# A longer warm-up and a new order of transforms, weight decodes and mixture steps in a one-core Fourier and MLP kernel

## The chip, the cores and the metric

The kernel runs on one core of a Trainium2 chip. The metric is the device time of one execution in microseconds, the median of several. A core has TensorE (PE, matmul), VectorE (DVE), ScalarE (ACT), GpSimd (POOL), SyncE (SP, which here issues the transfers) and 16 DMA engines.

## The reference, cut to what matters

For two batches of 3136 positions and 256 channels, in three parts:

```
X = rfft(x, axis=1)                                  # attention: a mixture in the Fourier domain
Yr, Yi = Xr@w_r - Xi@w_i + b_r, Xr@w_i + Xi@w_r + b_i
Y = sign(Y) * max(|Y| - 0.01, 0)                     # soft threshold, on both parts
y = irfft(Y, n=3136)
x1 = y + relu(layernorm(y) * g @ w_ch1) @ w_ch2      # first MLP, 256 -> 1024 -> 256
u = x1 + real(fft(fft(x1, axis=1), axis=2))          # second mixture
out = u + relu(layernorm(u) @ v_ch1) @ v_ch2         # second MLP
```

The weights of both MLPs arrive as 64-bit floating-point numbers, which the chip sees as integers.

## The kernel before, in words

The long transform is split into a contraction with 98 rows and short transforms of 64 points, and products that need more than the matmul's precision are made of a high and a low part (x h and x l), three matmuls each (L213 to L215, L219 to L221).

- **Forward** (class `Forward`, matmul L300, transpose L301): 16 groups of 512 columns for each batch. A group is one matmul with `cam`, two records in the trace, and one transpose by VectorE into `yg`. Batch 0 reads x through tiles h, batch 1 through tiles q. Ahead of all stand WARM_UP matmuls on zeros (L740).
- **Steps** (`p2_step`): 26 of them, 13 for each batch. `p2_b` makes the 64-point transform (L420) with the table `cb` and splits it into parts, `p2_mix` multiplies by `wm` (24 matmuls, L452) and applies bias and threshold (VectorE L458 and L459, then POOL L209), `p2_inv` transforms back (L472) with the table `cw`. `p2_mix` and `p2_inv` run some steps behind. STAGE1_AT says how many groups of batch 1's Forward stand in each step, STAGE3_AT how many groups of batch 0's Inverse, CONST_AT and MLP1_AT in which step a table is loaded and a weight piece decoded.
- **Inverse** (class `Inverse`): 16 groups for each batch: transpose by VectorE (L316), matmul (L318), copy by ACT (L201). After the last group the seven stores of dY follow (L324, L325), and the first MLP's loads of ya wait for them. Batch 1's groups run between tiles of the first MLP.
- **First MLP** (`run_mlp`, 13 chunks of 2 to 4 tiles): BN statistics (L549 to L551), normalization q (L562; POOL does some of it in chunk 0), transpose by TensorE with `ident` (L573) into psc and scaling (ACT L578, DVE L579), first layer (L219 to L221), activation (L597, L598), second layer (L213 to L215), sum with the input (L615), store dX. The prep of chunk 0 stands in the steps (PREP0_AT).
- **Second mixture** (class `Stage98`, one for each batch): `start` loads a middle column m and the first rows r, makes mhl (L204, L209) and mid, and splits two groups. Each of 16 `step`s loads a row group (L345), splits it on POOL (L357 to L359) and into s and its rest (ACT L201, DVE or POOL L209), multiplies (L219 to L221), and stores dA.
- **Second MLP**: 13 chunks, with `stage_b` (L674) and `dmix` (L699) as the second axis of the transform, weights `r2b`.
- **Weights**: `decode64` loads a piece of 512 KB (L489) and turns it into a high and a low part by eight VectorE operations (L495 to L503). There are eight pieces for each MLP; those of the second one are decoded during the first.

Within a program order that these tables set, a scheduler orders each engine's instructions by a simulated timeline. `hook` puts a function behind a given tile (chunk k, layer "l1" or "l2", tile i): decodes of the second weights (MLP2_AT, chunk and tile as the two digits), batch 1's inverse groups (STAGE3_MLP) and steps of the second mixture (STAGE4_FROM, STAGE4_AT). `s4[1]`, the mixture of batch 1, has a step behind each second-layer tile of chunks 0 to 3 of the second MLP.

Of the kernel before, what the change touches and what calls it, by code (L numbers as in the profile page):

```python
# [10 lines left out]
F32R = mybir.dt.float32r  # L11
I32 = mybir.dt.int32
# [3 lines left out]
YB, HB, WB, SB = 4, 9, 4, 2  # L16
R98, S98, O98 = 4, 8, 4


ZERO_AT = 12  # L20
STAGE1_AT = (0, 0, 0, 2, 2, 2, 2, 2, 2, 2, 2)
STAGE3_FROM = 16
STAGE3_AT = (0,) * 16 + (2, 2, 2, 2, 2, 2, 2, 2)
CONST_AT = (0, 0, 1, 2, 2, 3, 4, 5, 6, 8)
MLP1_AT = (5, 8, 10, 12, 13, 14, 15, 18)
MLP2_AT = (61, 65, 71, 75, 81, 85, 91, 95)
STAGE3_END = 3
STAGE3_MLP = ((0, 0), (0, 1), (0, 2), (0, 3), (1, 0), (1, 1), (1, 2), (1, 3),
              (2, 0), (2, 1), (2, 2), (2, 3), (3, 0))
# [1 line left out]
INV_BEHIND = 3  # L31
STAGE_B_AT = (1, 3)
DMIX_AT = (3, 5)
PREP0_AT = (26, 27)
L2_BEHIND = 7
PREP_BEHIND = (3, 2, 0)
APPLY_POOL = (0, 1)
APPLY_CHUNKS = 2
STAGE4_AT = ((7, "l2", 1), (7, "l2", 2), (7, "l2", 3), (8, "l1", 3), (8, "l1", 4), (8, "l2", 0),
             (8, "l2", 1), (8, "l2", 2), (8, "l2", 2), (9, "l1", 3), (9, "l2", 0), (9, "l2", 1),  # L40
             (9, "l2", 3), (10, "l1", 6), (10, "l2", 0), (10, "l2", 1), (10, "l2", 1), (10, "l2", 3))
STAGE4_FROM = (6, 4)
WARM_UP = 5
TB = 2
I64 = mybir.dt.int64
AF = mybir.ActivationFunctionType
# [115 lines left out]
def fourier_moe_kernel(ctx, tc, x, w_r, w_i, b_r, b_i, g_ln, w11, w12, w21, w22,  # L162
                       t_ca, t_cam, t_cim, t_cb, t_ci, t_cb0, t_ci0, t_cd, t_ident, out):
    nc = tc.nc
    sp = nc.sync

    cp = ctx.enter_context(tc.tile_pool(name="cp", bufs=1))
    wk = ctx.enter_context(tc.tile_pool(name="wk", bufs=2))
# [5 lines left out]
    def psum(tag):  # L174
        return pp.tile([128, 512], F32, tag="ps" + tag, name="ps" + tag, bufs=ps_bufs[tag])
# [24 lines left out]
    def a_copy(o, i, scale=1.0):  # L200
        nc.scalar.activation(out=o, in_=i, func=AF.Copy, scale=scale)  # L201
# [57 lines left out]
    wm = cp.tile([128, 2, 1024], F32R, tag="wm", name="wm")  # L259
# [5 lines left out]
    def behind(f):  # L265

        with ExitStack() as es:
            for k, ins in mark.items():
                if k != "pe":
                    es.enter_context(tc.issue_after(ins))  # L270
            f()
# [209 lines left out]
        p2_inv(i - INV_BEHIND)  # L481


    def decode64(src3, dh, dl, tag):


        s64 = wk.tile([128, 512], I64, tag=tag, name="s64", bufs=2)
        o = s64 if len(src3.shape) == 2 else s64.rearrange("p (f c) -> p f c", f=src3.shape[1])
        sp.dma_start(out=o, in_=src3)  # L489
        t = wk.tile([128, 2, 512], I32, tag="stg", name="t64", bufs=SB)  # L490
        w, low = s64.bitcast(I32)[:, 1::2], s64.bitcast(U32)[:, 0::2]
        t1, t2 = t[:, 0, :], t[:, 1, :]
# [12 lines left out]
    def load_mlp(w1, w2, r, tag):

        def piece(src, o):
            def f():
                decode64(src, r[:, 0, o:o + 512], r[:, 1, o:o + 512], tag)
            return f  # L510

        fs = []
        for i in range(4):
            c, h = divmod(i, 2)
            fs.append(piece(w1[c * 128:(c + 1) * 128, h * 512:(h + 1) * 512], i * 512))
        for i in range(4):
            fs.append(piece(w2[i * 256:(i + 1) * 256, :].rearrange("(f p) c -> p f c", p=128), 2048 + i * 512))
        return fs

    def w_views(r):  # L520
        return ([r[:, i, 0:2048].rearrange("p (k f) -> p k f", k=2) for i in range(2)],
                [r[:, i, 2048:].rearrange("p (f c) -> p f c", f=NF) for i in range(2)])
# [233 lines left out]

    def split_wm():
        for m in range(2):
            ms = slice(m * 512, (m + 1) * 512)
            a_copy(wm[:, 0, ms], wm_raw[:, ms])  # L760
            sub(nc.vector, wm[:, 1, ms], wm_raw[:, ms], wm[:, 0, ms])

    def l_bias():
        for h, bv in enumerate((b_r, b_i)):
            sp.dma_start(out=bias[h * 64:(h + 1) * 64].rearrange("p (u c) -> p u c", u=2),
                         in_=bv.unsqueeze(0).unsqueeze(0).broadcast_to([64, 2, D]))

# [12 lines left out]
    wv1 = w_views(r3)  # L780
    mlp1_w = load_mlp(w11, w12, r3, "o")
    todo = {}

    def l_ca():
# [31 lines left out]
    for i in range(NS + INV_BEHIND):  # L816
        for f in todo.get(i, ()):
            behind(f)
        for _ in range(STAGE1_AT[i] if i < len(STAGE1_AT) else 0):
            if fw[1].g % 2 == 0 and fw[1].g < 10:  # L820
                fw[1].load(fw[1].g // 2 + 3)
            fw[1].step()
        for _ in range(STAGE3_AT[i] if i < len(STAGE3_AT) else 0):
            inv[0].step()
        p2_step(i)
        if inv[0].g == 16 and y_ring is None:
            y_ring = y_spaces()
            mlp1[0].load()
            mlp1[1].load()
        if i == PREP0_AT[0]:  # L830
            mlp1[0].prep()
        if i == PREP0_AT[1]:
            mlp1[0].trans()
# [33 lines left out]
                    h()  # L867

    inv1 = lambda: inv[1].step()
    r2b = cp.tile([128, 2, 4096], F32R, tag="u0", name="r2b")  # L870
    wv2 = w_views(r2b)
    plan2 = [[((0, 4 * i + 2), (0, 4 * i + 1)), ((0, 4 * i + 4), (0, 4 * i + 3))] for i in range(6)]
    plan2 += [[((1, 2), (1, 1)), ((0, 0), (1, 0))]]
# [1 line left out]
    plan2 += [[((1, 24), (1, 23))]]  # L875
    mlp2 = chunks2(plan2, wv2)

    s98_ring = ring(cp.tile([128, S98 * 512], F32R, tag="u1", name="s98"), S98, 512)
    o98_ring = ring(cp.tile([128, O98 * 512], F32, tag="wm", name="o98"), O98, 512)
    s4 = [Stage98(dX1[b], dA2[b], ca_h, ca_l, "c") for b in range(NB)]  # L880
    hooks = {}

    def after(k, i, f):

        def g():
            with tc.issue_after(mlp1[k].rest[i]):
                f()
        return g

    def hook(k, part, i, f):  # L890
        hooks.setdefault((k, part, i), []).append(f)

    for k, f in enumerate(load_mlp(w21, w22, r2b, "stg")):
        hook(MLP2_AT[k] // 10, "l1", MLP2_AT[k] % 10, after(MLP2_AT[k] // 10, MLP2_AT[k] % 10, f))
    for k, i in STAGE3_MLP:
        hook(k, "l2", i, inv1)
    hook(7, "l1", STAGE4_FROM[0], s4[0].start)
    for k, part, i in STAGE4_AT:
# [3 lines left out]
    hook(0, "l1", STAGE4_FROM[1], s4[1].start)
    for k in range(4):
        for i in range(4):
            hook(k, "l2", i, s4[1].step)
# [32 lines left out]
```

## Time and profile before

| | us |
|---|---|
| median of 3 runs (859.79 to 861.05) | 859.82 |
| the profiled execution's own time | 862.04 |
| its span in the trace | 860.3 |
| TensorE busy, of the span | 827.9 (96%) |
| VectorE busy | 526.4 (61%) |
| ScalarE busy | 288.8 (34%) |
| GpSimd busy | 134.1 (16%) |

The profile of one execution gives, for every instruction, when it started, how long it took, and what ended the idle time of its engine before it. The granted clock of TensorE (PEclk) is 1.00 at full speed. Busy time tells which engine has the most work; in which stretch an engine that carries the kernel stands idle, and for whom, has to be read from the stretches themselves.

### The profile page before, as it was taken

Reading aid. Unit: us, or ns where it says so; the run is one execution under the profiler, and the core shown is the slowest. Engines: PE = TensorE matmul, PEld = TensorE weight load, DVE = VectorE, ACT = ScalarE, POOL = GpSimd, SP = SyncE. Lnnn points to the kernel's source line nnn. Section 1 sums busy time; section 2 is a strip of 40 time slices with the busy share of each in tenths; the row PEclk is TensorE's granted clock in tenths of the full one; section 3 lists DMA queues with packets and bytes.
Section 4 is the critical chain, followed back from the end, with each engine's and each line's share of the span. In section 5 each row is a group of like instructions: output and inputs, shape, how many; then the busy total and the mean of one; then the engine's idle time right before and its main releaser. Section 6 shows DMA issues by size and latency. Waiting matters only on the chain.

```text
span 860.3 us, 13553 instructions
## 1 busy us (share of the span) xinstructions
PE 827.9 (96%) x5235; PEld 724.6 (84%) x5235; DVE 526.4 (61%) x1190; ACT 288.8 (34%) x563; POOL 134.1 (16%) x184
## 2 busy tenths in 40 slices
PE   8899999979999999978999999899999999999997
PEld 3678977948888999967889997788899899999996
DVE  5578997356664545959764366476456656445652
ACT  0232356434443122243342234244432323322321
POOL 0012312221000000089410005244120000000000
PEclk9999999989999999989999999999999999999999
DMA  8733210440001600353423014333322122210001
GB/s 221 189 92 109 74 50 2 150 150 1 26 25 65 211 22 21 101 188 119 145 96 103 25 47 115 113 105 112 115 64 88 46 65 62 75 50 21 17 21 30
DMA packets 47923, 71.65 MB, mean 83 GB/s; under 512 B 11716, under 2 KB 32204, under 8 KB 47664
## 3 DMA queue, kind: packets, MB, share of 16 engines
q1 hardware_dynamic: 47860, 70.80, 27.1%
q8 instruction: 41, 0.67, 0.3%
q14 instruction: 22, 0.18, 0.1%
HBM read 45.09 MB, written 25.69 MB: 82 GB/s over the span
## 4 chain that ended last, share of the span: by engine, by line
PE 76%; DVE 9%; DMA 8%; SPq 2%; POOL 1%; issue 1%; ACT 1%; POOLq 0%; ACTq 0%
PE psb L213 10%; PE psb L215 10%; PE psb L214 10%; PE psa L219 9%; PE psa L220 9%; PE psa L221 9%; PE psb L452 5%; PE psc L318 3%; PE psc L573 2%; PE psc L674 2%; DMA r<-dX 2%; PE psa L420 2%; PE psc L300 1%; PE psc L472 1%; DMA cb<-in_cb_dram 1%
## 5 line engine op out<-in xcount | busy, mean ns | idle before, releaser
L597 ACT ACTIVATE h<-psa 128x512 fp32r<-128x512 f32 (+2 forms) x208 | 118.5, 573 | 267.0 <-PE psa L221 250.0
L598 DVE SCALAR_TENSOR_TENSOR h<-psa,h 128x512 fp32r<-128x512 f32 (+2 forms) x208 | 135.7, 654 | 105.2 <-ACT h L597 104.0
L213 PE MATMUL psb<-r3a,h 128*128 128x256 f32 x392 | 111.6, 288 | 2.3 <-DVE o L615 2.3
L213 PE MATMUL psb<-r2b,h 128*128 128x256 f32 x392 | 111.3, 287 | 0.0
L214 PE MATMUL psb<-r3a,h 128*128 128x256 f32 x392 | 110.4, 285 | 0.0
L214 PE MATMUL psb<-r2b,h 128*128 128x256 f32 x392 | 110.4, 284 | 0.0
L215 PE MATMUL psb<-r3a,h 128*128 128x256 f32 x392 | 109.4, 285 | 0.6 <-DVE h L598 0.6
L215 PE MATMUL psb<-r2b,h 128*128 128x256 f32 x392 | 107.7, 285 | 0.0
L452 PE MATMUL psb<-wm,h 128*128 128x256 f32 (+1 forms) x600 | 87.3, 297 | 0.0
L219 PE MATMUL psa<-q,r3a 128*128 128x512 f32 (+2 forms) x208 | 85.1, 409 | 2.1 <-ACT q L578 1.6
L219 PE MATMUL psa<-q,r2b 128*128 128x512 f32 (+2 forms) x208 | 82.3, 396 | 0.4 <-DVE h L598 0.4
L452 PEld LDWEIGHTS psb<-wm,h 128*128 128x128 f32 (+1 forms) x600 | 75.9, 189 | 7.3 <-issue 6.8
L220 PE MATMUL psa<-q,r3a 128*128 128x512 f32 (+2 forms) x208 | 79.6, 383 | 0.0
L615 DVE TENSOR_TENSOR o<-psb,yb 128x256 f32<-128x256 f32 x74 | 30.8, 422 | 79.6 <-PE psb L215 79.6
L221 PE MATMUL psa<-q,r3a 128*128 128x512 f32 (+2 forms) x208 | 78.9, 383 | 0.0
L213 PEld LDWEIGHTS psb<-r3a,h 128*128 128x128 f32 x392 | 75.7, 193 | 3.7 <-DVE o L615 2.5
L221 PE MATMUL psa<-q,r2b 128*128 128x512 f32 (+2 forms) x208 | 78.7, 379 | 0.0
L220 PE MATMUL psa<-q,r2b 128*128 128x512 f32 (+2 forms) x208 | 78.7, 378 | 0.0
L214 PEld LDWEIGHTS psb<-r3a,h 128*128 128x128 f32 x392 | 75.6, 193 | 1.2 <-issue 0.5
L213 PEld LDWEIGHTS psb<-r2b,h 128*128 128x128 f32 x392 | 75.6, 193 | 0.8 <-DVE o L615 0.2
L214 PEld LDWEIGHTS psb<-r2b,h 128*128 128x128 f32 x392 | 75.7, 193 | 0.4
L215 PEld LDWEIGHTS psb<-r3a,h 128*128 128x128 f32 x392 | 75.2, 193 | 0.8 <-DVE h L598 0.8
(108 smaller groups left out, 1424.7 us busy)
## 6 DMA issues: line engine op xcount, KB each, us to landing
s<-in_moe_w_ch_dram SPq DMA_DIRECT2D x16, 512.0 KB
r<-dX SPq DMA_DIRECT2D x32, 196.0 KB
dA<-o SPq DMA_DIRECT2D x32, 196.0 KB
dY<-yg SPq DMA_DIRECT2D x12, 512.0 KB
r<-dA SPq DMA_DIRECT2D x48, 128.0 KB
dX<-o SPq DMA_DIRECT2D x11, 512.0 KB
yb<-dX SPq DMA_DIRECT2D x50, 64.0 KB
out_dram<-o SPq DMA_DIRECT2D x50, 64.0 KB
```

Of the source, the lines that this page charges most:

```text
L213: nc.tensor.matmul(out=ps, lhsT=lh, rhs=rh, start=first, stop=False)
L214: nc.tensor.matmul(out=ps, lhsT=lh, rhs=rl, start=False, stop=False)
L215: nc.tensor.matmul(out=ps, lhsT=ll, rhs=rh, start=False, stop=last)
L219: nc.tensor.matmul(out=ps, lhsT=lh, rhs=rh, start=first, stop=False)
L220: nc.tensor.matmul(out=ps, lhsT=ll, rhs=rh, start=False, stop=False)
L221: ins = nc.tensor.matmul(out=ps, lhsT=lh, rhs=rl, start=False, stop=last)
L318: nc.tensor.matmul(out=ps[0:NQ, :], lhsT=cim, rhs=t, start=True, stop=True)
L420: nc.tensor.matmul(out=pa[:, 2 * u + c], lhsT=yg[b][:, k1 + u, c * 128:(c + 1) * 128], rhs=cb[:, k1 + u, :], start=True, stop=True)
L452: nc.tensor.matmul(out=ps[0:m, u * D:(u + 1) * D], lhsT=xv[:, o:o + m], rhs=wm_hl[wv][:, e, c, :], start=k == 0, stop=k == 11)
L597: nc.scalar.activation(out=h[:, 0:n], in_=ps[:, 0:n], func=AF.Relu)
L598: ins = nc.vector.scalar_tensor_tensor(out=l[:, 0:n], in0=ps[:, 0:n], scalar=0.0, in1=h[:, 0:n], op0=ALU.max, op1=ALU.subtract)
L615: nc.vector.tensor_tensor(out=self.o[:, i, :], in0=ps[:, 0:D], in1=self.y[:, i, :], op=ALU.add)
```

## The change

Eight tables and constants and a few lines change; what is computed does not. (Lines in the new kernel stand 3 to 22 further down: L300 becomes L303, L420 L423, L452 L455, L472 L475, L316 L319, L549 L569, L562 L582, L598 L618, L615 L635, L209 L212, L489 L491.)

- WARM_UP is 10 instead of 5. Batch 1's Forward begins at step 4 instead of 3. The first piece of `cb` is loaded as two, the second behind weights and bias. The low part of `wm` is made on GpSimd instead of VectorE.
- Inverse of batch 0 runs three groups a step instead of two (steps 16 to 21 instead of 16 to 23), and the prep of chunk 0 stands in steps 24 and 25.
- `decode64` is cut in `load64` and `decode64`; for the second weights the load is issued one piece ahead, the scratch is two tiles of another pool, and the pieces are decoded in chunks 4, 5, 5, 6, 6, 7, 9 and 10 instead of 6, 6, 7, 7, 8, 8, 9 and 9.
- The second mixture of batch 0 starts behind the first tile of chunk 7's second layer, of batch 1 two first-layer tiles later than before, and their steps follow new tables.

```diff
-STAGE1_AT = (0, 0, 0, 2, 2, 2, 2, 2, 2, 2, 2)
+STAGE1_AT = (0, 0, 0, 0, 2, 2, 2, 2, 2, 2, 2, 2)
-STAGE3_AT = (0,) * 16 + (2, 2, 2, 2, 2, 2, 2, 2)
+STAGE3_AT = (0,) * 16 + (3, 3, 3, 3, 3, 1)
-MLP2_AT = (61, 65, 71, 75, 81, 85, 91, 95)
+MLP2_AT = ((4, 6), (5, 2), (5, 6), (6, 2), (6, 6), (7, 3), (9, 3), (10, 6))
-PREP0_AT = (26, 27)
+PREP0_AT = (24, 25)
...
+STAGE4_AT = ((7, "l2", 3), (8, "l1", 1), (8, "l1", 3), (8, "l1", 5), (8, "l2", 0), (8, "l2", 1), (8, "l2", 2),
...
+STAGE4_MLP2 = ((0, "l2", 2), (0, "l2", 3), (1, "l1", 3), (1, "l2", 0), (1, "l2", 1), (1, "l2", 2), (1, "l2", 3),
...
-STAGE4_FROM = (6, 4)
-WARM_UP = 5
+STAGE4_FROM = ((7, "l2", 0), (0, "l1", 6))
+WARM_UP = 10
...
-            sub(nc.vector, wm[:, 1, ms], wm_raw[:, ms], wm[:, 0, ms])
+            sub(nc.gpsimd, wm[:, 1, ms], wm_raw[:, ms], wm[:, 0, ms])
...
-    l_cb(1, 4)
+    l_cb(1, 2)
     l_wm()
     l_bias()
+    l_cb(3, 2)
     l_ci(0, 4)
     for i in range(16):
         fw[0].step()
-    behind(split_wm)
+    split_wm()
...
+        def ask(k):
+            if k < 8 and k not in raw:
+                raw[k] = load64(srcs[k][0], tag)
+
+        def piece(k):
+            def f():
+                ask(k)
+                if two:
+                    ask(k + 1)
+                    t1, t2 = (wk.tile([128, 512], I32, tag="t98", name="t64", bufs=TB) for _ in range(2))
+                else:
+                    t = wk.tile([128, 2, 512], I32, tag="stg", name="t64", bufs=SB)
+                    t1, t2 = t[:, 0, :], t[:, 1, :]
+                o = srcs[k][1]
+                decode64(raw[k], r[:, 0, o:o + 512], r[:, 1, o:o + 512], t1, t2)
+            return f
...
+    mlp2_w = load_mlp(w21, w22, r2b, "stg", True)
+    hook(4, "l1", 2, mlp2_w[0])
+    for (k, i), f in zip(MLP2_AT, mlp2_w[1:]):
+        hook(k, "l1", i, after(k, i, f))
```

How the rows move is shown at three places. The first is the start on TensorE, behind the warm-up: h and cam are batch 0's forward groups, q and cam batch 1's, cb the 64-point transform, wm the mixing, cw the way back. Before:

```order
L300 MATMUL psa<-h,cam 128x512 x16
L420 MATMUL psa<-cb,yg_84 128x128 x2
L300 MATMUL psc<-q,cam 128x512 x2
L420 MATMUL psa<-cb,yg_84 128x128 x10
L452 MATMUL psb<-wm,h 128x256 x8
L420 MATMUL psa<-cb,yg_84 128x128 x4
L452 MATMUL psb<-wm,h 128x256 x40
L420 MATMUL psa<-cb,yg_84 128x128 x6
L452 MATMUL psb<-wm,h 128x256 x16
L472 MATMUL psc<-h,cw 128x256 x2
```

and with the change:

```order
L303 MATMUL psa<-h,cam 128x512 x16
L423 MATMUL psa<-cb,yg_84 128x128 x12
L455 MATMUL psb<-wm,h 128x256 x8
L423 MATMUL psa<-cb,yg_84 128x128 x4
L455 MATMUL psb<-wm,h 128x256 x40
L423 MATMUL psa<-cb,yg_84 128x128 x6
L455 MATMUL psb<-wm,h 128x256 x16
L475 MATMUL psc<-h,cw 128x256 x2
L303 MATMUL psc<-q,cam 128x512 x2
```

The two q groups that stood behind the first two cb matmuls are gone from there, and the first ones now come behind the first cw matmuls.

The second is VectorE around the prep of chunk 0 (h is the split of a 64-point transform, w a threshold, st, mv, sm and q the normalization). Before:

```order
L549 BN_STATS st<-ya 128x6 x4
L551 BN_AGGR mv<-st 128x2 x4
L458 TENSOR_TENSOR w<-psb,cw 128x512
L555 RECIPROCAL sm<-sm 128x4
L459 TENSOR_SCALAR w<-w 128x512
L556 SCALAR_TENSOR_TENSOR sm<-mv,sm 128x4
L458 TENSOR_TENSOR w<-psb,cw 68x256
L557 SCALAR_TENSOR_TENSOR sm<-sm 128x4
L459 TENSOR_SCALAR w<-w 68x256
L558 RECIPROCAL sm<-sm 128x4
L562 TENSOR_SCALAR q<-ya,mv,sm 128x256 x2
```

and with the change:

```order
L569 BN_STATS st<-ya 128x6 x4
L571 BN_AGGR mv<-st 128x2 x2
L461 TENSOR_TENSOR w<-psb,cw 128x512
L571 BN_AGGR mv<-st 128x2 x2
L462 TENSOR_SCALAR w<-w 128x512
L575 RECIPROCAL sm<-sm 128x4
L576 SCALAR_TENSOR_TENSOR sm<-mv,sm 128x4
L577 SCALAR_TENSOR_TENSOR sm<-sm 128x4
L578 RECIPROCAL sm<-sm 128x4
L582 TENSOR_SCALAR q<-ya,mv,sm 128x256 x2
L461 TENSOR_TENSOR w<-psb,cw 128x512
L462 TENSOR_SCALAR w<-w 128x512
```

Statistics and normalization now stand ahead of two more thresholds. On GpSimd, which makes two tiles of q and the last part of each threshold (h), q stands in the new order ahead of the last two h.

The third is VectorE in chunk 8, where the second mixture of batch 0 has begun (t and r2b are a weight decode, s is the mixture's split, o the sum behind the second layer). Before:

```order
L503 SCALAR_TENSOR_TENSOR r2b<-t_3535 128x512
L558 RECIPROCAL sm<-sm 128x4
L598 SCALAR_TENSOR_TENSOR h<-psa,h 128x512
L562 TENSOR_SCALAR q<-yb,mv,sm 128x256 x4
L495 TENSOR_SCALAR t_3616<-s_3614 128x512
L498 TENSOR_SCALAR t_3616<-s_3614 128x512
L497 SCALAR_TENSOR_TENSOR t_3616<-s_3614,t_3616 128x512
L615 TENSOR_TENSOR o<-psb,yb 128x256
L499 SCALAR_TENSOR_TENSOR r2b<-t_3616 128x512
L615 TENSOR_TENSOR o<-psb,yb 128x256
L209 TENSOR_TENSOR s_1649<-w,s_1649 98x512
```

and with the change:

```order
L575 RECIPROCAL sm<-sm 128x4
L576 SCALAR_TENSOR_TENSOR sm<-mv,sm 128x4
L577 SCALAR_TENSOR_TENSOR sm<-sm 128x4
L618 SCALAR_TENSOR_TENSOR h<-psa,h 128x512
L578 RECIPROCAL sm<-sm 128x4
L582 TENSOR_SCALAR q<-yb,mv,sm 128x256 x4
L618 SCALAR_TENSOR_TENSOR h<-psa,h 128x512 x3
L212 TENSOR_TENSOR s_1655<-w,s_1655 98x512
L635 TENSOR_TENSOR o<-psb,yb 128x256 x2
L599 SCALAR_TENSOR_TENSOR q<-psc,g_sb,q 128x512 x2
L635 TENSOR_TENSOR o<-psb,yb 128x256 x2
```

The decode's operations are no longer between the normalization and the sums o.

## Rows read from the trace of the kernel before

**Rows 1.** Busy time by stretch: length, PE, PEld, DVE, ACT, POOL, granted clock, DMA share, GB/s.

```profile
174.10:181.60 7.50, 1.74 (x5) 0.89 (x4) 5.74 (x18) 1.38 (x3) 3.45 (x4) 0.86 0.93 351
181.60:186.30 4.70, 4.56 (x13) 2.46 (x13) 2.48 (x3) 1.70 (x3) 1.18 (x1) 0.50 0.06 19
190.00:360.00 170.00, 170.00 (x1078) 150.81 (x1077) 101.36 (x243) 57.36 (x96) 2.47 (x2) 1.00 0.16 56
360.00:375.40 15.40, 10.80 (x87) 9.99 (x86) 10.80 (x30) 3.83 (x9) 5.63 (x8) 0.96 0.59 147
375.40:381.00 5.60, 5.60 (x14) 4.31 (x15) 3.79 (x5) 2.89 (x5) 5.60 (x9) 0.51 0.70 209
400.00:410.00 10.00, 6.95 (x41) 6.24 (x40) 9.79 (x15) 2.49 (x5) 10.00 (x12) 0.83 0.25 60
520.00:530.00 10.00, 7.93 (x45) 6.60 (x44) 5.29 (x16) 3.84 (x9) 3.56 (x6) 1.00 0.58 126
530.00:550.00 20.00, 17.78 (x113) 15.81 (x112) 14.99 (x30) 7.46 (x15) 12.89 (x20) 0.91 0.34 97
```

**Rows 2.** In order of time, start: start, us, engine, line, tiles, [idle before <-releaser].

```profile
1.13 2.31 PE L740 MATMUL psc<-wz 128*128 128x512 bf16 x5 [1.13 <-POOL wz L736]
...
4.19 3.75 PE L300 MATMUL psa<-h,cam 98*128 98x512 f32 x4 [0.75 <-DMA h<-in_x_dram]
...
8.83 15.65 PE L300 MATMUL psa<-h,cam 98*128 98x512 f32 x28 [0.88 <-DMA h<-in_x_dram]
...
15.93 9.89 DVE L301 STREAM_TRANSPOSE yg<-psa 128x512 f32<-128x512 f32 x11 [0.54 <-PE psa L300]
...
28.64 3.19 PE L300 MATMUL psc<-q,cam 98*128 98x512 f32 x4 [3.15 <-DMA q<-in_x_dram]
```

**Rows 3.** The chain of waits, start: start, us, what.

```profile
45.30 1.73 PE psc L300 x4
```

**Rows 4.** The chain of waits, 150 to 190.

```profile
154.33 1.97 ACT yg L201 x2
...
165.08 6.41 DMA dY<-yg
...
173.68 6.44 DMA ya<-dY
180.12 1.47 POOL q L562
```

**Rows 5.** In order of time, 360 to 430.

```profile
369.75 0.43 DVE L495 TENSOR_SCALAR t<-s 128x512 int32<-128x512 int32 x1 [2.39 <-DMA s<-in_moe_w_ch_dram]
...
372.89 0.45 PE L219 MATMUL psc<-s,ca_hl 98*98 98x512 f32 x1 [3.01 <-DVE mid L204]
...
375.39 0.79 PE L219 MATMUL psa<-q,r3a 128*128 128x512 f32 x1 [1.59 <-ACT q L578]
...
398.30 3.31 DVE L562 TENSOR_SCALAR q<-yb,mv,sm 128x256 f32<-128x256 f32 x4
...
404.32 0.39 PE L213 MATMUL psb<-r3a,h 128*128 128x256 f32 x1 [2.33 <-DVE o L615]
...
428.37 1.37 DVE L562 TENSOR_SCALAR q<-yb,mv,sm 128x256 f32<-128x256 f32 x4
```

**Rows 6.** In order of time, 515 to 548.

```profile
525.21 0.23 PE L213 MATMUL psc<-mhl,ca_hl 98*98 98x32 f32 x1 [1.80 <-DVE mhl L204]
...
538.89 4.13 DVE L562 TENSOR_SCALAR q<-yb,mv,sm 128x256 f32<-128x256 f32 x4
```

**Rows 7.** Groups by line: line, engine, operation, tiles, count, busy, mean ns, idle before.

```profile
L209 POOL TENSOR_TENSOR h<-w 128x512 f32<-128x512 f32 (+1 forms) x26 | 34.1, 1313 | 144.9 <-DVE w L459 99.5 <-ACT h L201 15.6 <-PE psc L300 12.2
L316 DVE STREAM_TRANSPOSE t<-yg 128x512 f32<-128x512 f32 x32 | 34.1, 1080 | 6.5 <-PE psc L318 3.3 <-ACT yg L201 3.2
...
L318 PE MATMUL psc<-t,cim 128*98 128x512 f32 x64 | 32.7, 605 | 0.3 <-DVE t L316 0.2
```

**Rows 8.** Busy time of VectorE on the decode's tile t, by stretch.

```profile
378.00:398.50 20.50, 6.52 (x8) 0.93 0.54 175
```

More of the change, by code (lines that the diff above doesn't have):

```diff
@@ L38 @@
 APPLY_CHUNKS = 2
-STAGE4_AT = ((7, "l2", 1), (7, "l2", 2), (7, "l2", 3), (8, "l1", 3), (8, "l1", 4), (8, "l2", 0),
-             (8, "l2", 1), (8, "l2", 2), (8, "l2", 2), (9, "l1", 3), (9, "l2", 0), (9, "l2", 1),
-             (9, "l2", 3), (10, "l1", 6), (10, "l2", 0), (10, "l2", 1), (10, "l2", 1), (10, "l2", 3))
-STAGE4_FROM = (6, 4)
-WARM_UP = 5
+STAGE4_AT = ((7, "l2", 3), (8, "l1", 1), (8, "l1", 3), (8, "l1", 5), (8, "l2", 0), (8, "l2", 1), (8, "l2", 2),
+             (8, "l2", 3), (9, "l1", 1), (9, "l1", 5), (9, "l2", 0), (9, "l2", 1), (9, "l2", 3),
+             (10, "l1", 1), (10, "l1", 3), (10, "l2", 0), (10, "l2", 1))
+STAGE4_MLP2 = ((0, "l2", 2), (0, "l2", 3), (1, "l1", 3), (1, "l2", 0), (1, "l2", 1), (1, "l2", 2), (1, "l2", 3),
+               (2, "l1", 3), (2, "l2", 0), (2, "l2", 1), (2, "l2", 2), (2, "l2", 3),
+               (3, "l1", 3), (3, "l2", 0), (3, "l2", 1), (3, "l2", 2))
+STAGE4_FROM = ((7, "l2", 0), (0, "l1", 6))
+WARM_UP = 10
 TB = 2
@@ L481, in p2_step, with load64 @@
         p2_inv(i - INV_BEHIND)
-    def decode64(src3, dh, dl, tag):
+    def load64(src3, tag):
         s64 = wk.tile([128, 512], I64, tag=tag, name="s64", bufs=2)
@@ L489, in decode64 @@
         sp.dma_start(out=o, in_=src3)
-        t = wk.tile([128, 2, 512], I32, tag="stg", name="t64", bufs=SB)
+        return s64
+    def decode64(s64, dh, dl, t1, t2):
         w, low = s64.bitcast(I32)[:, 1::2], s64.bitcast(U32)[:, 0::2]
-        t1, t2 = t[:, 0, :], t[:, 1, :]
         t1f, t2f = t1.bitcast(F32), t2.bitcast(F32)
@@ L503, in decode64, with load_mlp @@
         v.scalar_tensor_tensor(out=dl, in0=t2f, scalar=2.0 ** -20, in1=t1f, op0=ALU.mult, op1=ALU.mult)
[L505 to L512, printed above, removed]
+    def load_mlp(w1, w2, r, tag, two):
+        srcs, raw = [], {}
         for i in range(4):
             c, h = divmod(i, 2)
-            fs.append(piece(w1[c * 128:(c + 1) * 128, h * 512:(h + 1) * 512], i * 512))
+            srcs.append((w1[c * 128:(c + 1) * 128, h * 512:(h + 1) * 512], i * 512))
         for i in range(4):
-            fs.append(piece(w2[i * 256:(i + 1) * 256, :].rearrange("(f p) c -> p f c", p=128), 2048 + i * 512))
-        return fs
+            srcs.append((w2[i * 256:(i + 1) * 256, :].rearrange("(f p) c -> p f c", p=128), 2048 + i * 512))
+        def ask(k):
[13 more added lines that the diff above has]
+            return f
+        return [lambda: ask(0)] + [piece(k) for k in range(8)]
     def w_views(r):
@@ L776, in fourier_moe_kernel @@
         fw[0].step()
-    behind(split_wm)
+    split_wm()
     r3 = cp.tile([128, 2, 4096], F32R, tag="r3", name="r3a")
     wv1 = w_views(r3)
-    mlp1_w = load_mlp(w11, w12, r3, "o")
+    mlp1_w = load_mlp(w11, w12, r3, "o", False)[1:]
     todo = {}
@@ L869, in fourier_moe_kernel @@
     inv1 = lambda: inv[1].step()
-    r2b = cp.tile([128, 2, 4096], F32R, tag="u0", name="r2b")
+    r2b = cp.tile([128, 2, 4096], F32R, tag="u1", name="r2b")
     wv2 = w_views(r2b)
@@ L876, in fourier_moe_kernel @@
     mlp2 = chunks2(plan2, wv2)
-    s98_ring = ring(cp.tile([128, S98 * 512], F32R, tag="u1", name="s98"), S98, 512)
+    s98_ring = ring(cp.tile([128, S98 * 512], F32R, tag="u0", name="s98"), S98, 512)
     o98_ring = ring(cp.tile([128, O98 * 512], F32, tag="wm", name="o98"), O98, 512)
@@ L891, in hook @@
         hooks.setdefault((k, part, i), []).append(f)
-    for k, f in enumerate(load_mlp(w21, w22, r2b, "stg")):
-        hook(MLP2_AT[k] // 10, "l1", MLP2_AT[k] % 10, after(MLP2_AT[k] // 10, MLP2_AT[k] % 10, f))
+    mlp2_w = load_mlp(w21, w22, r2b, "stg", True)
+    hook(4, "l1", 2, mlp2_w[0])
+    for (k, i), f in zip(MLP2_AT, mlp2_w[1:]):
+        hook(k, "l1", i, after(k, i, f))
     for k, i in STAGE3_MLP:
         hook(k, "l2", i, inv1)
-    hook(7, "l1", STAGE4_FROM[0], s4[0].start)
+    hook(*STAGE4_FROM[0], s4[0].start)
     for k, part, i in STAGE4_AT:
@@ L901, in fourier_moe_kernel @@
     hooks = {}
[L902 to L905, printed above, removed]
+    hook(*STAGE4_FROM[1], s4[1].start)
+    for at in STAGE4_MLP2:
+        hook(*at, s4[1].step)
     run_mlp(mlp2, [], hooks)
```

## The prediction

> **What bounds the kernel now.** I read the page first, then the busy time of each engine by stretches, then the chain of waits and the order of time in the stretches that stood out. TensorE carries the kernel: in the long middle of the first MLP it is busy 170.00 of 170.00 us [rows 1], and no tuning of another engine can win anything there. So only stretches in which it idles, or runs at the lower of its two clock levels, can pay. They are four.
>
> (1) The start. Sixteen matmuls of batch 0's forward transform take 15.65 us from 8.83 on, the eleven last transposes on VectorE run 9.89 us back to back until 25.82, and then TensorE waits 3.15 us for x of batch 1 (q) before a group of 4 records that takes 3.19 us [rows 2]; the same group takes 1.73 us at 45.30, so at 28.64 the clock was on its lower level [rows 3]. It was there at first too: 4 records took 3.75 us and 28 took 15.65, where 0.43 each (1.73 / 4) would be 1.7 and 12.1.
>
> (2) The change from inverse transform to MLP. [...] The chain here is ACT's copy of the last inverse group, the stores of y, 6.41 us for the last, the load back, 6.44 us, and the normalization on POOL [rows 4].
>
> (3) The start of the second mixture on batch 0: 10.80 busy of 15.40 us before 375.4, then 5.60 us at a clock of 0.51, then 6.95 busy of 10.00 us from 400 [rows 1]. Rows in order of time say why. VectorE waits 2.39 us in a weight decode (L495) whose load was issued late; TensorE then waits 3.01 us for "mid", which is queued behind that decode on VectorE, and 1.59 us for ACT's q. The normalization L562 takes 3.31 us at 398.30, and TensorE waits 2.33 us for o behind another decode [rows 5].
>
> (4) The same mixture on batch 1: 7.93 of 10.00 us from 520, then 17.78 of 20.00 at a clock of 0.91 [rows 1], with a wait of 1.80 us for mhl and an L562 of 4.13 us [rows 6].
>
> **The change part by part.** The sum is made against the profiled execution (span 860.3, own time 862.04, 2.2 above the median of 859.82); the gains are then taken from the median.
>
> *Start: longer warm-up, batch 1's transform from step 4, cb in two pieces, low half of wm on POOL.* Batch 1's first group no longer stands between the first DFT matmuls and the rest, so neither its wait (3.15) nor its low clock (3.19 less 1.73, 1.46) is met there. The five more warm-up matmuls cost 5 x 0.46 = 2.3 us (2.31 for x5), which puts the first real matmul from 4.19 to about 5.75, but they fill the time in which TensorE waited for x (0.75 and 0.88 us), so it is busy from 1.13 on without a gap. In the trace of before the clock came up only in the run of 28 without a gap, and the lower level cost 2.0 + 3.5 = 5.5 us up to there. I expect it some 5 us earlier, which wins back 3.2 of these, and the transposes, 0.90 us each when they follow one another, then end near 22.6 instead of 25.82. From 31.83 (28.64 + 3.19) to 45.30 the same DFT and mixing work takes 13.47 us; with 0.5 for the four records that were already done, it ends at 22.6 + 14.0 = 36.6. The transfers set a bound of their own: they are the same bytes, q landed at 28.6, and pieces of cb are now wanted earlier; I add 1.4 and take 38.0. Before, that state stood at 45.30 - 1.73 = 43.57. Gain **5.6**, between 3 (clock as late as before) and 7.5 (no wait for cb). WM's low half on POOL, beside transposes, ends nothing.
>
> *Inverse of batch 0 three groups a step, prep of chunk 0 two steps earlier.* From 154.33 to the first ident matmul (180.12 + 1.47 + 0.05 = 181.64) the chain takes 27.3 us [rows 4]. In the new order the last inverse group comes 1 us of TensorE work earlier against that matmul, and POOL does q ahead of two of its thresholds (1.31 us for a full one, and an estimated 0.7 for the last, which has half the columns [rows 7]) instead of behind them. So the stall of 5.76 us (7.50 less 1.74) shrinks by 1.0 + 2.0 to about 2.8; but the thresholds then stand behind a q of 1.47 us and hold back the inverse matmuls that wait for them, and the low clock behind the stall (4.7 us at 0.50, so 2.35 lost) I leave. Gain 1.0 + 2.0 - 1.47 = **1.5**; between -1 (the q moved ahead only swaps the two waits, and three transposes in a row on VectorE, 1.08 us each [rows 7], hold back a threshold) and 5.
>
> *Second mixture on batch 0: decodes spread over chunks 4 to 10 with loads one ahead, start a hook later.* No decode is left in chunk 8. The 2.39 us in which VectorE stood in front of a missing load go, and with them the 3.01 us of TensorE; of the 4.60 us lost before 375.4 I leave 0.8 for q behind ACT's s, as its POOL split is there still. The low clock that followed (5.60 us at 0.51, 2.74 lost) goes with the stall. In 378 to 398.5 one decode's eight operations took 6.52 us of VectorE [rows 8]; that, and the part of the next one in 400 to 410, frees the queue in which L562 and o stood, so of the 3.05 us lost there and of the clock of 0.83 (1.7 us) 1.0 is left: 3.75. Gain 3.8 + 2.74 + 3.75 = **10.3**; between 5 (the stall and its clock stay, but for a bit over 1 us) and 12.1 (all of it).
> That L562 is slow here is the row's: 3.31 us at 398.30 with POOL busy, 1.37 us for the same four at 428.37 with POOL idle [rows 5]. [...]
>
> *The same on batch 1: steps on a table of hooks instead of every second-layer tile.* The wait for mhl (1.80) stays: the middle column is stored, loaded and cast as before. Lost in 520 to 550 are 2.07 + 2.22 us, and 1.8 by the clock of 0.91, 6.1 in all; of the 4.3 that are not mhl's I take half. Gain **2.0**, between 0 and 4.3.
>
> *Decodes in chunks 4 to 7.* Five pieces come into the stretch 190 to 360, where VectorE is busy 101.36 of 170.00 us [rows 1]; five more at 6.52 at most make 134. Cost 0, covered by that idle time; at worst a decode holds back TensorE once as it did o at 404.32 (2.33 us [rows 5]), so -2.3.
>
> *Sum:* 5.6 + 1.5 + 10.3 + 2.0 + 0 = **19.4 us**, 859.8 - 19.4 = **840.4**. All low ends together: 3 - 1 + 5 + 0 - 2.3 = 4.7 us, 855.1. All high ends: 28.9 us, 830.9.
>
> **Rivals.**
> - *The stall at the second mixture stays.* For it: the chain dX stored, m loaded, cast, multiplied, copied is no shorter, and ACT's q stands behind s and POOL's split. Against it: the trace names a decode as what mid stood behind. Then part three gives 3.75 only: 5.6 + 1.5 + 3.75 + 2.0 = 12.9, time 846.9. Chance 0.18.
> - *VectorE and POOL in turns.* Two of the normalizations, for chunks 9 and 10, still fall among splits and cost 3.31 - 1.37 = 1.94 each, 3.9 where I left 1.0. For it: both rows of L562 above and the 4.13 at 538.89. Against it: with no decode, a late L562 has more slack. Gain 16.5, time 843.3. Chance 0.12. [...]
> - *The clock comes up no sooner.* Then the start gives 3.15 + 1.46 less 1.56 for the later first matmul and 1.5 for cb, 1.5: sum 15.3, time 844.5. Chance 0.12.
> - *Nothing is late in the new order.* Parts two to four give their high ends: 5.6 + 5 + 12.1 + 4.3 = 27.0, time 832.8. Chance 0.10.
> - *Slower: VectorE becomes the bound of the inverse stage.* Three transposes a step are 3.2 us of VectorE beside its thresholds and BN work, in steps whose TensorE work is shorter for it. If TensorE waits for each of the 16 groups, that is 16 x 1.08 = 17.3 us, and four falls of the clock like that of 181.6 (2.35 each) are 9.4 more: 840.4 + 26.7 = 867.1. It decides once waits and clock together pass 19.4 us, 1.2 a group. Against it: at two a step, TensorE waited for these transposes 0.2 us in all 32 groups [rows 7]. Chance 0.05.
> - The low ends fall together and no change can be told: 0.03.
>
> **How the numbers follow.** My forecast, 840.4, has 0.40; the rest is above. A measurement of this kernel tells some 0.2%, 1.7 us, from no change. Range: 832 (nothing late) to 853 (the start at its low end with the stall of the first rival kept: 859.8 - 3 - 0 - 3.75 = 853); outside lie the slower rival, the low ends together and part of the best case. All cases but the last two are faster: 0.92; within 0.2% 0.03; slower 0.05.
>
> **What would show it.** Right: no wait for q in the first 40 us and a group of batch 1 at 1.73 us when it first runs; the clock up before 12; first ident matmul after a stall of about 3 us; no decode row between the s rows of chunk 8, "mid" copied within 1 us of its matmuls, no clock of 0.51 there; 580 to the end unchanged in length. Wrong: a granted clock of 0.5 in new places, L562 of over 3 us with TensorE waiting behind it, transposes L316 that TensorE waits for, or a DVE queue that stands before a weight load in chunks 4 to 10.

## The result and the profile after

The changed kernel took 845.57 us (844.21 to 847.87, 4 runs) where the kernel before took 860.43 beside it: a ratio of 0.9828, 95% interval 0.9802 to 0.9854, 14.9 us less. Forecast were 840.4 us and 19.4 us. The number lies in the range of 832 to 853, the direction is right, and so is the place of each gain; one term of the sum, the largest, was three times too big.

To see where the time came from, the table has the same events in both traces: when VectorE starts the eleventh threshold add (L458, then L461), and when it starts the first activation remainder (L598, then L618) of a chunk. Differences of two such marks are the lengths of the stretches.

| stretch, us | before | change | gain | forecast |
|---|---|---|---|---|
| start, to the eleventh threshold | 97.43 | 91.48 | 5.95 | 5.6 |
| from there to chunk 2 of the first MLP | 146.74 | 145.43 | 1.31 | 1.5 |
| from there to chunk 0 of the second MLP | 274.53 | 271.16 | 3.37 | 10.3 |
| from there to the end | 341.57 | 337.99 | 3.58 | 2.0 |
| span | 860.3 | 846.1 | 14.2 | 19.4 |

The start in order of time, with the group of batch 1 that answers to [rows 2] at its end:

```profile
1.13 3.67 PE L760 MATMUL psc<-wz 128*128 128x512 bf16 x10 [1.13 <-POOL wz L756]
...
4.64 1.88 PE L303 MATMUL psa<-h,cam 98*128 98x512 f32 x4
...
8.58 13.02 PE L303 MATMUL psa<-h,cam 98*128 98x512 f32 x28 [2.06 <-DMA h<-in_x_dram]
...
23.54 4.30 PE L423 MATMUL psa<-cb,yg 128*128 128x128 f32 x22 [1.73 <-DMA cb<-in_cb_dram]
...
38.46 1.88 PE L303 MATMUL psc<-q,cam 98*128 98x512 f32 x4
```

The first four records take 1.88 us instead of 3.75, as long as the four at 38.46, where the granted clock is 1.00; by that the clock is up after the ten warm-up matmuls; but then TensorE waits 2.06 us for x where it waited 0.88. The wait for q is gone, a shorter one for cb (1.73) has come, and batch 1's first group follows the first way back at full clock (1.00).

Busy time around the end of batch 0's inverse and in the second mixture on batch 0 (columns as in [rows 1]):

```profile
166.20:172.80 6.60, 1.62 (x13) 1.40 (x13) 5.81 (x17) 0.78 (x2) 2.71 (x3) 1.00 0.99 382
172.80:178.00 5.20, 5.05 (x18) 3.79 (x19) 2.45 (x5) 2.34 (x4) 3.30 (x3) 0.67 0.05 18
...
380.00:390.00 10.00, 4.64 (x28) 3.62 (x26) 9.89 (x12) 2.83 (x5) 9.44 (x19) 0.98 0.54 166
...
390.00:395.00 5.00, 4.96 (x30) 4.96 (x31) 2.20 (x4) 0.00 (x0) 3.05 (x6) 0.70 0.13 40
```

The first two lines answer to the stall and low clock of 174.1 to 186.3 [rows 1]: 4.98 us idle instead of 5.76, then 5.2 us at 0.67 instead of 4.7 at 0.50. The third line was not forecast. TensorE stands still for more than half of 380 to 390, with both VectorE and POOL nearly full. What happens there, in order of time, VectorE first and then TensorE:

```profile
380.29 1.31 DVE L576 SCALAR_TENSOR_TENSOR sm<-mv,sm 128x4 f32<-128x4 f32 x1
...
382.51 6.87 DVE L582 TENSOR_SCALAR q<-yb,mv,sm 128x256 f32<-128x256 f32 x4
389.31 1.87 DVE L618 SCALAR_TENSOR_TENSOR h<-psa,h 128x512 fp32r<-128x512 f32 x3
```

```profile
382.45 0.50 PE L222 MATMUL psa<-q,r3a 128*128 128x512 f32 x1 [1.51 <-DVE h L618]
...
390.04 0.58 PE L218 MATMUL psb<-r3a,h 128*128 128x256 f32 x1 [3.89 <-DVE h L618]
```

The waits for mid (3.01) and for o (2.33) of [rows 5] are gone, as forecast. In their place TensorE waits 1.51 and 3.89 us for h. The h of the first wait stands on VectorE behind a remainder s and L576, which takes 1.31 us here and 0.16 by the median of its 26 executions. The h remainders of the second wait stand behind the normalization L582, whose four operations take 6.87 us; they took 3.31 in the kernel before and 1.37 with POOL idle [rows 5].

### The profile page after: what moved, and what is told of

Same layout as the page of the kernel before. It is cut to its first block, busy times and chain, and to the rows that moved or that the text cites. A ratio compares the mean times of both kernels' runs of the same rounds, so it can differ in the third digit from the quotient of the medians.

```text
span 846.1 us, 13573 instructions
## 1 busy us (share of the span) xinstructions
PE 818.9 (97%) x5240; PEld 721.6 (85%) x5240; DVE 523.7 (62%) x1188; ACT 288.8 (34%) x563; POOL 127.6 (15%) x186
## 4 chain that ended last, share of the span: by engine, by line
PE 81%; DVE 6%; DMA 6%; POOL 2%; SPq 2%; issue 1%; ACT 1%; POOLq 0%; ACTq 0%
PE psb L218 11%; PE psb L216 11%; PE psb L217 11%; PE psa L222 10%; PE psa L224 10%; PE psa L223 10%; PE psb L455 4%; PE psc L321 3%; PE psc L694 2%; PE psc L593 2%; PE psa L423 2%; PE psc L303 2%; DMA h<-in_x_dram 2%; PE psc L475 1%; PE psa L719 1%
## 5 line engine op out<-in xcount | busy, mean ns | idle before, releaser
L618 DVE SCALAR_TENSOR_TENSOR h<-psa,h 128x512 fp32r<-128x512 f32 (+2 forms) x208 | 135.0, 654 | 100.0 <-ACT h L617 98.9
L455 PE MATMUL psb<-wm,h 128*128 128x256 f32 (+1 forms) x600 | 89.3, 298 | 2.9 <-DVE mv L571 2.9
L222 PE MATMUL psa<-q,r3a 128*128 128x512 f32 (+2 forms) x208 | 84.2, 405 | 2.8 <-DVE h L618 1.7
L455 PEld LDWEIGHTS psb<-wm,h 128*128 128x128 f32 (+1 forms) x600 | 76.4, 189 | 10.8 <-issue 10.2
L635 DVE TENSOR_TENSOR o<-psb,yb 128x256 f32<-128x256 f32 x74 | 30.8, 422 | 82.3 <-PE psb L218 82.2
L223 PE MATMUL psa<-q,r3a 128*128 128x512 f32 (+2 forms) x208 | 78.9, 379 | 0.0
L224 PE MATMUL psa<-q,r3a 128*128 128x512 f32 (+2 forms) x208 | 77.8, 379 | 0.0
```

Of the source, the lines that this page charges most:

```text
L222: nc.tensor.matmul(out=ps, lhsT=lh, rhs=rh, start=first, stop=False)
L223: nc.tensor.matmul(out=ps, lhsT=ll, rhs=rh, start=False, stop=False)
L224: ins = nc.tensor.matmul(out=ps, lhsT=lh, rhs=rl, start=False, stop=last)
L455: nc.tensor.matmul(out=ps[0:m, u * D:(u + 1) * D], lhsT=xv[:, o:o + m], rhs=wm_hl[wv][:, e, c, :], start=k == 0, stop=k == 11)
L618: ins = nc.vector.scalar_tensor_tensor(out=l[:, 0:n], in0=ps[:, 0:n], scalar=0.0, in1=h[:, 0:n], op0=ALU.max, op1=ALU.subtract)
L635: nc.vector.tensor_tensor(out=self.o[:, i, :], in0=ps[:, 0:D], in1=self.y[:, i, :], op=ALU.add)
```

## The experiments

The runs are beside one another in three groups, in which the kernel before took 863.65 to 864.26 us, 3 to 4 more than beside the result. The times expected below were set against the result. So ratios to the kernel before are compared, and stretches of the traces as in the table above. The start differs by 2 to 4 us between traces of the same code: the eleventh threshold is at 91.48 in the trace shown, at 89.44 in the next one and at 87.80 in that of e9_q_act2, and at 97.43 and 94.99 in two traces with the start of the kernel before.

**The changed kernel again, a2_change.** 

> The changed kernel again, beside the next three. Every theory: the stall of 3.9 us behind L582 in chunk 8 again, 1.0 to 1.2% less time than e3_q_act gains left over, and the start within 2 us of the first trace, since its transfers vary.

Measured: 846.07 us, ratio 0.9800 (0.9764 to 0.9835). The wait behind L582 is there again with 3.8 us and L582 with 6.80. The stretch from chunk 2 to the second MLP takes 272.68 us here, and 271.92, 272.57 and 272.85 in the three runs below that leave its order alone (e5_inv2, e6_s1_3, e4_warm5), against 274.53 and 275.02 in two traces of the kernel before's order. So what the change gains there is 1.7 to 3.9 us, by which pair of traces one takes. The ratio lies 0.7% over that of e3_q_act, the next kernel, not the 1.0 to 1.2% that I expected (with the first ratio, 0.9828, it is 1.0%).

**Chunk 9's normalization on ScalarE, e3_q_act.**

```diff
+                if self in mlp1[9:10]:
+                    nc.scalar.activation(out=self.yn[:, i, :], in_=y[:, i, :], func=AF.Identity,
+                                         scale=r[:, i:i + 1], bias=nb[:, i:i + 1])
+                    continue
                 eng = nc.gpsimd if i in APPLY_POOL and self in mlp1[0:APPLY_CHUNKS] else nc.vector
```

> The changed kernel, but the normalization q of the first MLP's chunk 9 (four operations, L582, 6.87 us on VectorE at 382.51 while POOL is busy) is made by ScalarE. Theory: VectorE's L582 and POOL's splits lock one another out, and the second activation step (L618), queued behind L582, holds TensorE 1.5 and 3.9 us and then lets its clock fall. Expected: both waits under 0.5 us, 5 to 7 us gained on the change, 838.5 to 840.5, the stretch from chunk 7 to chunk 10 as much shorter. Rival: POOL's splits pace the mixture and TensorE would wait for s or o instead: under 1.5 us gained, waits for s in the place of those for h.

Measured: 841.12 us, ratio 0.9729 (0.9685 to 0.9774). The time is 0.6 over what I expected, in a group in which the kernel before took 3.8 more than beside the result. The order in chunk 8 is the same but for the four operations, a small one on VectorE that makes their bias (L581), and one matmul of the mixture that stands elsewhere. The four take 2.08 us on ScalarE:

```profile
381.89 2.08 ACT L586 ACTIVATE q<-yb,sm 128x256 f32<-128x256 f32 x4 [3.38 <-DVE sm L581]
```

The wait of 3.89 us is gone, no stretch at the lower clock follows (the granted clock is 1.00 from 380 to 393), and chunk 2 to second MLP takes 266.08 us, 5.1 less than in the first trace of the change and 6.6 less than in the second, as expected. The wait of 1.5 us stayed (1.54): that h stands behind L576 and an s, which is not what was moved; there my expectation was wrong. The rival, POOL's pace, would have put a wait for s in this place; none came.

**Without POOL's splits, e7_no_split.**

```diff
+            if self.dst is s4_dst0:
+                h, l = s98()
+                a_copy(h, t)
+                sub(nc.gpsimd if g % 3 > 0 else nc.vector, l, t, h)
...
+                return
```

> The changed kernel, but batch 0's second mixture leaves out the sums and differences on POOL (the split L360 to L362): s is made from r directly, so batch 0's mixture is of other numbers. If POOL's splits are what makes L582 slow, the four in chunk 8 take 1.4 to 2.5 us in place of 6.87, the wait of 3.9 us for h goes and so does that of 1.5: 5 to 8 us gained between chunk 7 and chunk 11. Rival, that VectorE's queue is late by its own work: L582 still waits its turn, under 2 us gained.

Measured: 838.74 us, ratio 0.9721 (0.9682 to 0.9761); chunk 2 to second MLP 262.13 us, 9.0 and 10.6 less than the two traces of the change and more than the 5 to 8 I expected. The same four operations on VectorE, with one s and one h more ahead of them in its queue:

```profile
376.67 1.37 DVE L589 TENSOR_SCALAR q<-yb,mv,sm 128x256 f32<-128x256 f32 x4
```

6.87 us have become 1.37, and both waits for h are gone. POOL, which still makes some of the remainders s, is idle here from 376.08 on. So VectorE's queue was not late by its own work; what made L582 long was POOL's work beside it. In the change each of the four operations (1.09, 2.90, 1.49 and 1.63 us) ends 0.15 us after a sum or difference of POOL's ends, the second only after the third of them in a row. POOL lost little by it: in the change its sums and differences beside L582 took 0.72 us each, where the median of all is 0.73, and the three copies there (L362) 0.25 to 0.26 us, where it is 0.20; in the kernel before they took up to 0.88 beside L562 at 398.30. By what the one engine holds up the other is not shown.

**Decodes where they were, e1_decode_old.**

```diff
-MLP2_AT = ((4, 6), (5, 2), (5, 6), (6, 2), (6, 6), (7, 3), (9, 3), (10, 6))
+MLP2_AT = ((6, 1), (6, 5), (7, 1), (7, 5), (8, 1), (8, 5), (9, 1), (9, 5))
```

(the first load goes to chunk 5 with it; loads one ahead and the new places of scratch, r2b and s stay). 

> The changed kernel with the second weights decoded at the hooks of the kernel before (chunks 6 to 9, two each), loads still one ahead. The prediction's reason (a decode stood before mid and before o): 6 to 10 us of what that stage won are lost, about 852 to 856. Rival, that the decodes only changed places with L582 as what VectorE is late with: 0 to 4 us lost, 845.5 to 849.5.

Measured: 849.16 us, ratio 0.9817 (0.9781 to 0.9853). The stretch takes 274.11 us, 1.3 to 3 more than in the change, in the rival's range and not in that of the prediction; the ratio alone does not tell it from the change. The waits in 340 to 425, by what was waited for, in this run:

```profile
PE psa L222 <- ACT q L598: 5.5, 1, 5.5
PE psc L593 <- DVE q L582: 1.9, 3, 1.1
PE psa L222 <- DVE h L618: 1.1, 1, 1.1
```

and in the change:

```profile
PE psb L218 <- DVE h L618: 3.9, 1, 3.9
PE psa L222 <- DVE h L618: 1.7, 2, 1.5
PE psa L222 <- ACT q L598: 1.1, 1, 1.1
```

The decode's place does matter: with it back, TensorE waits 5.5 us at the start of the mixture. But this is not what the prediction named: there is no wait for mid, and 0.3 us for o. ACT's q stands behind an s whose split on POOL waits for its row group r until 362.7, loaded behind a weight piece, and then takes 2.9 us beside the decode. With the decode away this wait is 1.1 us, but L582 takes 6.87 us instead of the 3.85 of this run. The one wait was sold for the other. POOL has no pause beside L582 in either trace; its sums and differences take 0.72 us each there in the change, and up to 1.87 beside the decode in this run. Why VectorE gets its turn less often in the change is not shown.

**Mixture starts and steps where they were, e2_mix_old.**

```diff
-STAGE4_FROM = ((7, "l2", 0), (0, "l1", 6))
+STAGE4_FROM = ((7, "l1", 6), (0, "l1", 4))
-STAGE4_MLP2 = ((0, "l2", 2), (0, "l2", 3), (1, "l1", 3), (1, "l2", 0), (1, "l2", 1), (1, "l2", 2), (1, "l2", 3),
...
+STAGE4_MLP2 = tuple((k, "l2", i) for k in range(4) for i in range(4))
```

(and STAGE4_AT as before). 

> The changed kernel with the second mixture's starts and steps at the hooks of the kernel before, for both batches. If the new tables are what took 3.5 us off the mixture of batch 1: that stretch loses 3 to 4 us; if that came from the state of TensorE and POOL at its start and not from the table, under 1. For batch 0: prediction's reason has the tables worth little there (0 to 2 us); the rival has the later start to thank for the missing wait for mid, 3 to 5 us. In all 848.5 to 854.

Measured: 852.12 us, ratio 0.9848 (0.9809 to 0.9887). From chunk 0 of the second MLP on it takes 341.77 us, as in the kernel before (341.57) and 3.8 more than the change: all of what batch 1's mixture gained comes from its new start and steps, which this edit takes back together. L580 takes 4.13 us there again, as it did in [rows 6], where the change's L582 in that place takes 2.23. That row is not what the gain hangs on: in e8_before_q_act, with the old hooks, it takes 2.21, and the stretch 342.42 us all the same. For batch 0 the stretch takes 275.04 us, 2.2 to 3.9 more than the change: with the decodes away and the old steps nothing at all is gained. By the trace of the change that one takes, this lies between the two expectations or in the rival's; but no wait for mid came back, as none did with the old decodes (e1_decode_old), and neither named the cause. Here one VectorE operation lasts longer beside POOL's work than the four of L582 did:

```profile
380.44 7.09 DVE L574 SCALAR_TENSOR_TENSOR sm<-mv,sm 128x4 f32<-128x4 f32 x1
```

This is an operation on four columns. The median of its 26 executions is 0.16 us. POOL has no pause from 377 to 387.6, and L574 ends at 387.53, as POOL's run ends; TensorE waits 7.30 us for the h behind it.

**Five warm-up matmuls, e4_warm5.**

```diff
-WARM_UP = 10
+WARM_UP = 5
```

> The changed kernel with 5 warm-up matmuls instead of 10. The prediction's reason (the longer warm-up brings the clock up earlier): the first 16 transposes end 2 to 3 us later, 847.5 to 849. Rival, that x's transfers set the pace of the start: within 0.5 us of the change in the trace, the clock still up by the time that the transfers allow.

Measured: 848.00 us, ratio 0.9806 (0.9768 to 0.9844), no loss: the time lies in the first range, but the ratio lies between the two of the change, and the eleventh threshold comes at 89.34 us, as in the change. Weight loads of the first transform tell the clock here, in order of time:

```profile
4.18 17.74 PE L303 MATMUL psa<-h,cam 98*128 98x512 f32 x32 [0.73 <-DMA h<-in_x_dram]
...
11.30 0.34 PEld L303 LDWEIGHTS psa<-h,cam 98*128 98x128 f32 x1 [0.52 <-issue]
11.88 0.19 PEld L303 LDWEIGHTS psa<-h,cam 98*128 98x128 f32 x1 [0.25 <-issue]
```

A load takes 0.34 us at the lower level, as in the kernel before at 29.92, where the granted clock is 0.50 (in the traces of the kernel before and of the change it is 1.00 or 0.50; the mean from 28.64 to 31.83 is 0.60), and 0.19 at the higher, as each of the 32 loads of q in the change, the first of which run at 1.00. By these loads the clock comes up between 11.3 and 11.9; the granted clock of the profile reads 1.00 on both sides of it and does not show this. The 32 records end at 21.92; in the change all ran at the higher level (0.19 us a load), and they ended at 21.60. So the longer warm-up does bring the clock up sooner, as I had it, and that is worth a few tenths, because x arrives no sooner: TensorE waits 2.06 us for a transfer instead. In the trace that I had worked from, the last slow load was at 14.96, and the last transpose ended at 25.82. With five warm-up matmuls as well, it ended at 23.18 in this run and at 22.04 in e8_before_q_act; with ten, at 22.76 and 22.28 in the two traces of the change. The 3.2 us that I expected from the clock were mostly a matter of that one trace.

**Batch 1's transform from step 3, e6_s1_3.**

```diff
-STAGE1_AT = (0, 0, 0, 0, 2, 2, 2, 2, 2, 2, 2, 2)
+STAGE1_AT = (0, 0, 0, 2, 2, 2, 2, 2, 2, 2, 2)
```

> The changed kernel with batch 1's forward transform from step 3, as before; warm-up still 10. The prediction's reason: the wait for q (3.15 us) and its group at the lower clock (1.46) come back, 3 to 4.6 us lost by the first mixing. Rival, that the loads of cb are what the start waits for anyway: under 1.5 us lost, a wait for q in place of that for cb.

Measured: 854.66 us, ratio 0.9904 (0.9873 to 0.9935). The eleventh threshold comes at 95.39 us, 3.9 and 5.95 later than in the two traces of the change, where 3 to 4.6 were expected. TensorE waits for q longer than in [rows 2]:

```profile
26.28 3.78 PE L303 MATMUL psc<-q,cam 98*128 98x512 f32 x4 [5.71 <-DMA q<-in_x_dram]
```

The order of the two batches is what the start gained by, nearly all of it: 5.55 us lie between the second traces of the two orders (94.99 and 89.44), and with ten warm-up matmuls and the new loads of cb the old order still gives 95.39.

**Inverse two groups a step, e5_inv2.**

```diff
-STAGE3_AT = (0,) * 16 + (3, 3, 3, 3, 3, 1)
+STAGE3_AT = (0,) * 16 + (2, 2, 2, 2, 2, 2, 2, 2)
-PREP0_AT = (24, 25)
+PREP0_AT = (26, 27)
```

> The changed kernel with two inverse groups a step and the prep of chunk 0 two steps later, as before. The prediction's reason: 1.5 us lost between the end of the start and chunk 1, stall and low clock at the first MLP as in the kernel before (5.8 us idle, then about 4.7 us at a granted clock of 0.5). Rival, that only the store and load back of y set that stretch, whatever the order in it: under 0.5 us.

Measured: 850.55 us, ratio 0.9842 (0.9791 to 0.9894). From the eleventh threshold to chunk 2 it takes 148.53 us, 3.1 more than the change (145.43) and 1.8 more than the kernel before. The wait is one again:

```profile
171.76 2.08 PE L475 MATMUL psc<-h,cw 128*128 128x256 f32 x4 [5.49 <-POOL h L212]
```

In the change it is two, 2.89 and 2.12 us, with 12 matmuls of the mixing between them. That is the forecast's reason, with a larger size in this run. What puts it 1.8 us over the kernel before, whose order it has in this stretch, stays open; a part may be the clock, 0.50 from 171.8 to 178.6, where [rows 1] have it so for 4.7 us. Its timed runs lie between 844.20 and 853.02, so the ratio does not tell it from the change, and the trace alone carries this reading.

**The kernel before with chunk 9's normalization on ScalarE, e8_before_q_act**, the same edit as e3_q_act. 

> The kernel before with chunk 9's normalization q (L562, 3.31 us at 398.30) made by ScalarE, nothing else changed. If there, too, L562 behind POOL's splits was what held the sums o (2.33 us) and q's transposes (0.73), 3 to 5 us are gained between chunk 8 and chunk 11, with the clock of 0.83 gone. If the decodes were what VectorE was late with, as the prediction had it, under 1.5 us.

Measured: 862.29 us, ratio 0.9979 (0.9959 to 0.9998). The stretch takes 275.02 us (274.53 before), so nothing is gained where L562 ran; the 0.2% of the ratio do not come from there. TensorE now waits 3.50 us for o instead of 2.33:

```profile
398.02 0.80 DVE L495 TENSOR_SCALAR t<-s 128x512 int32<-128x512 int32 x1 [1.54 <-DMA s<-in_moe_w_ch_dram]
...
402.01 0.41 DVE L623 TENSOR_TENSOR o<-psb,yb 128x256 f32<-128x256 f32 x1
```

The decode still stands ahead of o, and now it is first early enough to wait for its load. In the kernel before, the decode was the last thing that VectorE was late with, as the prediction read it; the normalization became that only when the decode had gone.

**Chunks 9 and 10 on ScalarE, e9_q_act2**, the edit of e3_q_act for two chunks. 

> The changed kernel with the normalizations of chunks 9 and 10 on ScalarE. Theory: TensorE waited for no L582 of chunk 10, so within 0.5 us of e3_q_act between chunks 7 and 12, 1.0 to 1.4% under the change; a rival that every VectorE operation beside POOL's splits costs TensorE time: another 1 to 2 us.

Measured: 841.69 us, ratio 0.9731 (0.9702 to 0.9761); the stretch takes 266.89 us, 0.8 more than e3_q_act, 0.3 outside what I expected, and no further gain. The ratio lies 0.7 and 1.0% under the change's, not 1.0 to 1.4%. e3_q_act is the fastest of the kernels that compute everything, with e9_q_act2 beside it; the change's ratios are 0.9800 and 0.9828. Of these only 0.9800 has an interval that touches that of e3_q_act, and neither touches that of e9_q_act2; the stretch of the trace in question is 4.3 to 6.6 us shorter in both than in the change.

## Why the prediction was right, and where its sum failed

- *Start, 5.6:* measured 5.95 in the two profiles and 5.55 in the second pair. The size was right, and half of its reason. The wait for q was the cause, and it was the larger where the transposes ended sooner (3.15 with them at 25.82, 5.71 in e6_s1_3). The clock did come up sooner with ten warm-up matmuls, but the matmuls that it makes cheaper end hardly sooner, at 21.60 instead of 21.92 (e4_warm5), since they wait for x; the 3.2 us that I counted for it belonged to the trace, not to the change. The wait for cb, 1.4 in the forecast, measured 1.73.
- *Inverse and first chunk, 1.5:* measured 1.3, and 3.1 by undoing it, of which 1.8 are not explained. The idle time shrank less than I had it (4.98 against 2.8 + 1.47), the low clock behind it also shrank (0.67 against 0.50).
- *Second mixture on batch 0, 10.3:* measured 3.4, with the repeats 1.7 to 3.9. This is the step that failed: "that, and the part of the next one in 400 to 410, frees the queue in which L562 and o stood, so of the 3.05 us lost there and of the clock of 0.83 (1.7 us) 1.0 is left". The waits for mid and o and the clock of 0.51 went, as forecast. But TensorE waits 5.6 us for h in their place, 3.9 of them behind L582, and then its clock falls again (0.70 in 390 to 395, 1.5 us). L582 was held up by more than its queue: the four operations rose from 3.31 to 6.87 us beside POOL's splits. The smaller part of the miss is the start of the mixture, where 0.8 us were to be left and 2.7 are, for q, o and s. In all TensorE is idle for 8.26 us from 340 to 425, and for 8.68 in the kernel before, so what was gained there is nearly all clock. The rival "VectorE and POOL in turns" had the cause, POOL's splits beside the normalization (1.37 us without them, e7_no_split), and was priced at 1.94 us a normalization, the difference of two rows; chunk 9's measured 5.5 (6.87 less 1.37), and chunk 10's 1.8 with nothing waiting behind it. Its time, 843.3, and the first rival's, 846.9, lie on either side of the result. The nearest, 844.5, is the clock rival's by luck: the start gave 5.95 and not its 1.5.
- *Second mixture on batch 1, 2.0:* measured 3.6, all of it by the new start and steps (e2_mix_old). TensorE waits 0.3 us for q instead of 2.6; the wait for mhl stays (1.56), as forecast. Of the 4.3 us that I halved, most went.
- *Decodes in chunks 4 to 7, 0:* nothing in the traces speaks against it; chunks 2 to 7 take the same time in both kernels (111.28 and 111.29 us from mark to mark).
- *Slower rival:* TensorE waited 0.2 us in all for the transposes of 32 inverse groups, at three a step as at two.
- *The number:* that it fell into the range owes something to luck. Start and batch 1 gave 1.9 us more than forecast where batch 0 gave 6.9 less. Two of the prediction's own signs of being wrong came true: a normalization of over 3 us with TensorE waiting behind it, and the lower clock in a new place.

## What to carry to other kernels

When an operation is slow beside a busy engine, its row need not be its price once the neighbour's work moves: the same four operations took 1.37, 3.31 and 6.87 us here. Before a change takes work off a late engine, ask which of the operations that are left took longer in the trace beside another engine's work, and whether a third engine can take them. And of a wait that is removed only the part counts that the next late thing does not take: the waits for o and for h had to go at once, by moving the decodes and then the normalization to ScalarE.

## What the runs showed of the hardware

Beside a run of GpSimd operations without a pause VectorE was served late, and not by the size of its work: an operation on four columns, 0.16 us by its median, lasted 7.09 us, to the end of the run (e2_mix_old). In the change L576, the same operation, got through within such a run after 1.31 us, and so did the four of L582, one by one. What decides after which GpSimd operation VectorE gets its turn is not shown. Activations on ScalarE beside the same splits took 2.08 us for the four, 0.52 each. I had not expected that an operation this small could hold TensorE for 7.30 us.
